# Linformer attention and an MLP mixer: next batch's front half in pieces between channel-mixing blocks, crossbar transposes, TensorE tiles

## The chip, the cores and the metric

One NeuronCore of one Trainium2 chip. The metric is device time in microseconds (us) of one execution, median over runs. PE is TensorE, ACT is ScalarE, DVE is VectorE, POOL is GpSimd, SP is SyncE. "SPq" in a profile line is SP's instruction queue. Matmul results go to tiles in PSUM; the ACT or DVE instruction that reads such a tile out is called its eviction. A crossbar transpose is `dma_start_transpose`, a DMA that transposes on its way.

## The reference, cut to what matters

Eight batches, S = 1024 tokens, 8 heads of 64, model width 512. Inputs are float32; the kernels work in bf16.

```
k_proj = E @ k ; v_proj = F @ v                  # per head, 1024 tokens -> 64 rows
x      = softmax(q @ k_proj.T / 8) @ v_proj      # heads side by side: 1024 x 512
h      = relu(x.T @ w_tok1) @ w_tok2             # token mixing: 1024 -> 256 -> 1024
u      = x + h.T
out    = u + relu(u @ w_ch1) @ w_ch2             # channel mixing: 512 -> 1536 -> 512
```

I call attention and token mixing the front half of a batch, channel mixing the back half.

## The kernel before

The front half of batch b+1 is written in front of the mixing of batch b. PSUM is one pool of eight banks.

```
psA = tile_pool(name="psA", bufs=8, space=PSUM)

def attention(b):
    ... loads of k, v, q, one DMA per head, POOL queue, float32 -> bf16 ...
    for hp in range(HP):                                 # q: copy, 64 TensorE transposes a batch ...
        nc.any.tensor_copy(out=q2_sb[:, hp], in_=q_sb[...])
    ...     nc.tensor.transpose(qt_ps[...], q2_sb[:, hp, si, :, :]..., ident)
    ...     nc.vector.tensor_copy(out=qT_sb[...], in_=qt_ps)
    for si in range(NSI):                                # v projection, 64 of 128 columns used
        nc.tensor.matmul(vproj_ps, FT_sb[:, si, :], v_sb[:, :, si, :], ...)
    for si in range(NSI):                                # then k projection
        nc.tensor.matmul(kproj_ps, ET_sb[:, si, :], k_sb[:, :, si, :], ...)
    for sj in range(2):
        for hp in range(HP):                             # scores: two 64x64 tiles at once, exp on ACT
            ...
        for hp in range(HP):                             # outputs and, in separate matmuls, denominators
            nc.tensor.matmul(dn_ps[...], lhs, bd_ones, ...)
            nc.tensor.matmul(ou_ps[:, ss, :], lhs, vbd_sb[:, hp, :], ...)
            ... reciprocal, multiply -> x_sb ...

def mixer(b, x_sb):
    ... token mixing: 16 + 16 matmuls of 512 columns; u_sb = u_ps + x_sb on DVE ...
    ... u: 32 TensorE transposes, evicted to uT_sb by DVE ...
    ... channel mixing: 96 matmuls -> gT_ps, relu; 96 matmuls -> g2_ps; add u, store ...

xs[0] = attention(0)
... weight loads, POOL queue ...
for b in range(B):
    if b + 1 < B:
        xs[b + 1] = attention(b + 1)
    mixer(b, xs[b])
```

The softmax here doesn't subtract the row's maximum and nothing guards it: scores larger than these inputs give would overflow.

## Time and profile before

571.1 us (median of 3 runs, 571.06 to 571.5).

The page of the kernel before: busy time of PE with its share and instruction count; then PE's busy share and the granted PE clock, in tenths, over 40 equal slices of 14.3 us.

```profile
PE 509.8 (89%) x3120; PEld 259.4 (45%) x3120; DVE 210.4 (37%) x524; ACT 175.9 (31%) x288; POOL 110.9 (19%) x212
...
PE   1540889999999999998999999999999999999997
...
PEclk9975889999999999999999999999999999999999
```

PE is the bound after the first six slices. In the first four it is mostly idle, and in slices three to six the granted clock is lowered (0.5 to 0.8).

The chain of waits of the kernel before, in order of time (start us, length us, what):

```profile
65.69 4.79 DMA q_sb<-in_q_dram
70.57 1.05 ACT q_sb L99
74.44 4.15 PE h_ps L198 x16
...
85.20 20.96 PE gT_ps L233 x96
106.16 20.73 PE g_ps L242 x96
126.92 0.69 DVE o_sb L247
...
149.83 20.96 PE gT_ps L233 x96
```

Channel mixing of batch 0 starts at 85.2 us, because PE meets the attention of batch 1 first and waits there for its q. From then on a batch takes 149.83 - 85.20 = 64.6 us, of which 41.7 are the two channel-mixing loops.

Stretches of the kernel before: the start, then one batch. Columns: stretch, its length, busy time and count for PE, PEld, DVE, ACT, POOL, then PE clock, DMA share (packet times of queues that overlap add up, so it can exceed 1), GB/s.

```profile
0.00:85.20 85.20, 40.72 (x345) 26.02 (x346) 33.85 (x107) 19.00 (x27) 56.91 (x110) 0.82 1.16 193
85.20:149.80 64.60, 62.69 (x390) 31.71 (x388) 25.76 (x64) 21.89 (x36) 15.28 (x29) 1.00 0.48 93
```

In one batch PE is busy 62.7 of 64.6 us. A faster batch therefore needs less PE work, not only better overlap.

### The profile page before, as it was taken

Reading aid. Unit: us, or ns where it says so; the run is one execution under the profiler, and the core shown is the slowest. Engines: PE = TensorE matmul, PEld = TensorE weight load, DVE = VectorE, ACT = ScalarE, POOL = GpSimd, SP = SyncE. Lnnn points to the kernel's source line nnn. Section 1 sums busy time; section 2 is a strip of 40 time slices with the busy share of each in tenths; the row PEclk is TensorE's granted clock in tenths of the full one; section 3 lists DMA queues with packets and bytes.
Section 4 is the critical chain, followed back from the end, with each engine's and each line's share of the span. In section 5 each row is a group of like instructions: output and inputs, shape, how many; then the busy total and the mean of one; then the engine's idle time right before and its main releaser. Section 6 shows DMA issues by size and latency. Waiting matters only on the chain.

```text
span 570.8 us, 7698 instructions
## 1 busy us (share of the span) xinstructions
PE 509.8 (89%) x3120; PEld 259.4 (45%) x3120; DVE 210.4 (37%) x524; ACT 175.9 (31%) x288; POOL 110.9 (19%) x212
## 2 busy tenths in 40 slices
PE   1540889999999999998999999999999999999997
PEld 0330454454544454445544454445544454445443
DVE  1440571137502572028602563027601563025012
ACT  0221336305260235304260235404261034500720
POOL 8608871006200360006200260000000000000000
PEclk9975889999999999999999999999999999999999
DMA  9999992129502390028601391020001200020012
GB/s 135 208 208 202 201 201 44 38 92 151 91 0 79 102 186 4 27 103 134 109 1 73 94 185 19 20 102 28 1 1 69 80 2 0 18 94 38 1 55 92
DMA packets 39555, 46.90 MB, mean 82 GB/s; under 512 B 4192, under 2 KB 30304, under 8 KB 39520
## 3 DMA queue, kind: packets, MB, share of 16 engines
q0 software_dynamic: 30304, 29.63, 32.4%
q1 hardware_dynamic: 9216, 16.78, 7.5%
q8 instruction: 24, 0.39, 0.3%
q14 instruction: 11, 0.09, 0.1%
HBM read 59.24 MB, written 16.78 MB: 133 GB/s over the span
## 4 chain that ended last, share of the span: by engine, by line
PE 71%; DVE 14%; DMA 6%; POOL 5%; issue 2%; ACT 1%; DVEq 0%; ACTq 0%; POOLq 0%
PE gT_ps L233 29%; PE g_ps L242 29%; DVE u_sb L213 6%; PE h_ps L198 5%; DMA wc_sb<-in_moe_w_ch_dram 4%; DVE qT_sb L114 2%; PE ou_ps L178 2%; PE ut_ps L219 2%; POOL v_sb L90 2%; POOL q_sb L94 2%; PE u_ps L209 2%; POOL k_sb L89 1%; DVE x_sb L183 1%; PE dn_ps L175 1%; DVE vbd_sb L128 1%
## 5 line engine op out<-in xcount | busy, mean ns | idle before, releaser
L233 PE MATMUL gT_ps<-uT_sb,wc_sb 128*128 128x512 bf16 x768 | 169.0, 379 | 0.0
L242 PE MATMUL g_ps<-wc_sb,gT_sb 128*128 128x512 bf16 x768 | 167.1, 379 | 0.0
L238 ACT ACTIVATE gT_sb<-gT_ps 128x512 bf16<-128x512 f32 x184 | 109.0, 597 | 111.6 <-PE gT_ps L233 110.5
L247 DVE TENSOR_TENSOR o_sb<-g_ps,u_sb 128x512 f32<-128x512 f32 x64 | 44.3, 692 | 267.7 <-PE g_ps L242 267.7
L242 PEld LDWEIGHTS <-gT_sb 128*128 128x128 bf16 x768 | 75.1, 98 | 90.7
L233 PEld LDWEIGHTS <-wc_sb 128*128 128x128 bf16 x768 | 74.8, 98 | 90.7 <-issue 3.8
L90 POOL DMA_DIRECT2D v_sb<-in_v_dram x64 | 34.7, 545 | 203.2 <-PE vproj_ps L120 188.5
L99 ACT COPY q_sb<-q_sb 128x1024 bf16<-128x1024 bf16 x23 | 23.1, 1044 | 133.8 <-PE qt_ps L109 109.8
L166 ACT ACTIVATE attnT_sb<-sco_ps 128x512 bf16<-128x512 f32 x64 | 33.0, 602 | 61.2 <-PE sco_ps L161 61.2
L109 PE MATMUL qt_ps<-ident,q_sb 128*128 128x128 bf16 x256 | 19.5, 242 | 34.4 <-ACT q_sb L99 34.4
L213 DVE TENSOR_TENSOR u_sb<-u_ps,x_sb 128x512 bf16<-128x512 f32 x64 | 39.0, 683 | 21.2 <-PE u_ps L209 21.2
L183 DVE TENSOR_TENSOR x_sb<-ou_ps,rdn 128x512 bf16<-128x512 f32 x64 | 41.7, 681 | 1.7
L89 POOL DMA_DIRECT2D k_sb<-in_k_dram x64 | 34.6, 554 | 14.9 <-DMA wc_sb<-in_moe_w_ch_dram 6.8
L94 POOL DMA_DIRECT2D q_sb<-in_q_dram x64 | 34.0, 534 | 10.1 <-issue 5.3
L109 PEld LDWEIGHTS <-q_sb 128*128 128x128 bf16 x256 | 17.6, 109 | 37.1 <-ACT q_sb L99 35.5
L114 DVE COPY qT_sb<-qt_ps 128x512 bf16<-128x512 bf16 x64 | 23.0, 417 | 19.2 <-PE qt_ps L109 19.1
L175 PE MATMUL dn_ps<-bd_ones,attnT_sb 128*128 128x2 bf16 x256 | 27.4, 171 | 2.8 <-ACT attnT_sb L166 1.5
L178 PE MATMUL ou_ps<-vbd_sb,attnT_sb 128*128 128x128 bf16 x256 | 29.8, 221 | 0.0
L198 PE MATMUL h_ps<-x_sb,wt_sb 128*128 128x512 bf16 x128 | 29.7, 386 | 0.0
L209 PE MATMUL u_ps<-hT_sb,wt_sb 128*128 128x512 bf16 x128 | 28.9, 379 | 0.0
L175 PEld LDWEIGHTS <-attnT_sb 128*128 128x128 bf16 x256 | 20.0, 96 | 16.2 <-ACT attnT_sb L166 10.8
L219 PE MATMUL ut_ps<-ident,u_sb 128*128 128x128 bf16 x256 | 21.5, 221 | 5.1 <-DVE u_sb L213 4.6
(46 smaller groups left out, 260.0 us busy)
## 6 DMA issues: line engine op xcount, KB each, us to landing
out_dram<-o_sb SPq DMA_DIRECT2D x64, 256.0 KB, 2.0
k_sb<-in_k_dram POOLq DMA_DIRECT2D x64, 128.0 KB, 4.9
v_sb<-in_v_dram POOLq DMA_DIRECT2D x64, 128.0 KB, 4.9
q_sb<-in_q_dram POOLq DMA_DIRECT2D x64, 128.0 KB, 4.9
wc_sb<-in_moe_w_ch_dram POOLq DMA_DIRECT2D x2, 1536.0 KB, 18.8
wt_sb<-in_moe_w_tok_dram POOLq DMA_DIRECT2D x2, 512.0 KB, 7.4
E_sb<-in_E_dram POOLq DMA_DIRECT2D x1, 128.0 KB, 3.1
F_sb<-in_F_dram POOLq DMA_DIRECT2D x1, 128.0 KB, 3.4
```

What stands on the lines that cost most here:

```text
L90: nc.gpsimd.dma_start(out=v_sb[:, h, :, :], in_=v[b, h].rearrange(rr, p=P))
L94: nc.gpsimd.dma_start(out=q_sb[:, h, :, :], in_=q[b, h].rearrange("(p si) d -> p si d", p=P))
L175: nc.tensor.matmul(dn_ps[:, 2 * ss : 2 * ss + 2], lhs, bd_ones, start=True, stop=True)
L178: nc.tensor.matmul(ou_ps[:, ss, :], lhs, vbd_sb[:, hp, :], start=True, stop=True)
L183: nc.vector.tensor_tensor(out=x_sb[:, sj * 4 : sj * 4 + 4, h0 * D : (h0 + 2) * D] .rearrange("p s (j d) -> p s j d", j=2), in0=ou_ps.rearr ...
L198: nc.tensor.matmul(h_ps, wt1_sb[:, sc, tc_i * P : (tc_i + 1) * P], x_sb[:, sc, :], start=(sc == 0), stop=(sc == SC - 1),)
L209: nc.tensor.matmul(u_ps, wt2_sb[:, tc_i, sc::NSI], hT_sb[:, tc_i, :], start=(tc_i == 0), stop=(tc_i == TC - 1),)
L213: nc.vector.tensor_add(out=u_sb[:, sc, :], in0=u_ps, in1=x_sb[:, sc, :])
L233: nc.tensor.matmul(gT_ps, wc1_sb[:, dc, cc * P : (cc + 1) * P], uT_sb[:, dc, s_lo : s_lo + S2], start=(dc == 0), stop=(dc == DMC - 1),)
L238: nc.any.tensor_relu(out=gT_sb[:, cc, s_lo : s_lo + S2], in_=gT_ps)
L242: nc.tensor.matmul(g2_ps, gT_sb[:, cc, sc * P : (sc + 1) * P], wc2_sb[:, cc, :], start=(cc == 0), stop=(cc == CC - 1),)
L247: nc.vector.tensor_add(out=o_sb, in0=g2_ps, in1=u_sb[:, sc, :])
```

## The change

Intent: cut the front half into 24 small units and issue one after every one or two blocks of four channel-mixing matmuls, so that their evictions hide; move the transposes of q and u from PE to the DMA crossbar; put the k and v projections in two column tiles that run at once and the scores in four 64x64 tiles; get the denominators from a column of ones in the output matmul. PSUM is split: three buffers for channel mixing (`psC`), two double ones for scores and outputs (`psA`), one for everything else (`psS`).

```diff
-    psA = tile_pool(name="psA", bufs=8, space=PSUM)
+    psC = tile_pool(name="psC", bufs=3, space=PSUM)
+    psA = tile_pool(name="psA", bufs=2, space=PSUM)     # two banks each
+    psS = tile_pool(name="psS", bufs=1, space=PSUM)
...
+    loaded = {0: load(0, 4)}          # k, v, q; POOL queue
+    ... weight loads ...
+    loaded[1] = load(1, 2)
...
-    nc.tensor.transpose(qt_ps[...], q2_sb[...], ident); nc.vector.tensor_copy(...)
+    def front_units(b):
+        for h in range(0, H, H // 2):                   # two transposes of 128x2048, on SP
+            nc.sync.dma_start_transpose(out=qT[:, h : h + H // 2]..., in_=q_sb[:, h : h + H // 2]...)
...
+        def kv_proj():
+            kv_ps = psS.tile([P, H, D], F32, tag="s", name="kv_ps")
+            for si in range(NSI):
+                nc.tensor.matmul(kv_ps[0:KP], ET_sb[:, si, :], k_sb[:, :, si, :], ...)
+                nc.tensor.matmul(kv_ps[KP : 2 * KP], FT_sb[:, si, :], v_sb[:, :, si, :], ...)
+        ... k_transpose, scores(hp), attend(h), token1(t) ...
+        def token2(si):
+            u_ps = psS.tile([P, DM], F32, tag="s", name="u_ps")
+            ... two matmuls, u_sb = u_ps + x_sb ...
+            if si % NJ == NJ - 1:                       # after the 4th and the 8th: on SP too
+                nc.sync.dma_start_transpose(out=uT[i]..., in_=u_sb[:, i * NJ : (i + 1) * NJ]...)
...
+    for unit in front_units(0):
+        unit()
     for b in range(B):
-        if b + 1 < B:
-            xs[b + 1] = attention(b + 1)
-        mixer(b, xs[b])
+        if b + 2 < B:
+            loaded[b + 2] = load(b + 2, 2)
+        units = front_units(b + 1) if b + 1 < B else []
+        blocks = back_blocks(b)                         # 48 blocks of 4 matmuls
+        first = 12 if b == 0 else 2
+        ... after each block, the units that are due ...
```

## The prediction

> **What bounds the kernel now.** TensorE. The page's first part has PE busy 509.8 us (89%) of 570.8, and the chain of waits is 71% PE, 14% DVE. In order of time the chain repeats every 64.6 us (from 126.9 to 191.5): the two channel-mixing loops 20.96 + 20.73 us (matmuls 216 ns apart); attention of the next batch 12.9; token mixing with the transposes of u 10.0. In the channel-mixing stretch PE is 100% busy, in the attention stretch 11.6 of 12.9 us, in token mixing 9.4 of 10. So little is idle: the gain must come from PE work removed, and from short bubbles. The first channel-mixing matmul starts only at 85.2 us, because PE meets attention(1) before mixing(0) in its order and waits there for q of batch 1 (the copy of it starts at 70.6); the clock is 0.67 to 0.71 there.
>
> **Costs, per batch, from the trace.**
> Removed: transposes of q 1.9 us and of u 2.2 us with their DVE bubbles (now DMA transposes); half of the k and v projections (they run one after the other, 3.6 us; in two column tiles 1.8); the denominator matmuls (a pair of denominator and output takes about 80 ns, a 130-column one alone about 60); waits for evictions in attention, about 1.3 us, and 0.6 in token mixing. The scores already run two 64x64 tiles at once (both start at 133.71); four quadrants halve 1.75 us to 0.9.
> Kept: 41.7 channel, 6.9 token mixing (32 x 216 ns).
> Estimate of the new batch: 41.7 + 6.9 + 1.8 (projections) + 0.6 (k transposed) + 0.9 to 1.7 (scores) + 2.4 (output) + about 1.2 for some ten changes of tile shape (0.1 us each, as between the last output matmul and the next score at 136.6) = 55.5 to 56.3 us instead of 64.6.
>
> **Will the transposes hide?** Each moves 128x2048 bf16, 512 KB. The Trainium skill ("DMA: Bandwidth & Descriptors", Latency and other measured facts) gives 261 GB/s for such a transpose, so about 2 us plus as much fixed; I estimate 4 to 8 us beside the loads; nothing in this trace shows it. In the instruction order the transposes of q stand nearly a batch ahead of their scores, and after the fourth token-mixing block some 11 us of matmuls come before the first that needs u transposed. So they should hide, except at the start.
>
> **Start.** Loads of k, v, q end near 20 us (weights follow until 43). Then q transposes, scores, eight output steps of about 1 us each (two buffers), token mixing with one buffer (8 x 1.4 us), and a transpose of u: channel mixing(0) should start near 53 us (48 to 60) instead of 85, since attention(1) now comes inside it.
>
> **Sum.** 53 + 7 x 56 + 42.5 (last batch has nothing between) + 3 = 490.5 us. Range 474 to 513. Faster by over 2%: 0.95; same 0.03; slower 0.02.
>
> **What would show it.** Period 55 to 57 us between the same blocks of successive batches; PE busy near 95% from 60 us on; channel matmuls still 216 ns apart; k and v projection pairs starting together; four scores starting together; PE's waits for transposed q only in the first batch, for transposed u under 1 us per batch; ACT near 45% with all the relus, not limiting.
>
> **What would make it wrong.** Transposes at 12 us or more each (four per batch), so that the first channel matmul waits each batch: up to 60 us per batch, 520 in all. The Trainium skill ("TensorEngine Tiling (Array Packing)", Key Properties) says that changing the tiling mode drains TensorE; if it costs 0.3 us rather than 0.1, 15 us more. One buffer for projections and token mixing stalling PE in order. A start held to 65 us or more by transposes queued behind the weight loads.

## The result, and the profile after

The changed kernel takes 520.0 us (median of 4 runs, 518.87 to 520.71) against 571.1 us for the kernel before (median of 4, the three runs above among them). The ratio is 0.910, 95% interval 0.909 to 0.911. Ratios here and below are the mean time of one kernel's runs over the mean of the other's runs of the same rounds, so not quite the ratio of the medians. Executions over 1.5% slower than the fastest of the same kernel are left out of the means. The change is clearly faster, but the time lies outside the predicted range of 474 to 513 us.

The page after, same lines as before (slices of 12.9 us):

```profile
PE 449.0 (87%) x2384; PEld 209.1 (40%) x2384; DVE 163.0 (31%) x300; ACT 163.2 (32%) x265; POOL 49.0 (9%) x72
...
PE   1300751999999999999999999999999999999997
...
PEclk9999975999999999999999999999999999999999
```

From slice eight on PE has no visible gap. The start has not become shorter, and it is emptier: PE is busy 24.4 us of its 88.1, against 40.7 of 85.2 before (the stretches below).

The chain of waits after:

```profile
12.05 9.96 DMA q_sb<-in_q_dram
...
22.29 19.96 DMA wc_sb<-in_moe_w_ch_dram
...
42.54 20.19 DMA q_sb<-in_q_dram
...
62.75 7.01 SPq L133
...
69.81 11.81 SPq L133
...
81.66 6.39 DMA uT_172<-u_sb
...
88.09 1.01 PE g_ps L254 x2
...
145.35 3.45 PE g_ps L254 x16
...
199.93 3.45 PE g_ps L254 x16
```

Read from the top: the loads of batch 0, then the weights, then q of batch 1 (landed at 62.7), then two instructions of line 133 on SP (the transposes of q), and only then the transpose of u that the first channel-mixing matmul needs. That matmul starts at 88.1 us, later than the 85.2 before. The steady state is as good as hoped: 199.93 - 145.35 = 54.6 us a batch.

Stretches after: start, batch 0, one steady batch, the last batch (same columns).

```profile
0.00:88.10 88.10, 24.40 (x119) 11.02 (x120) 16.76 (x39) 7.79 (x10) 27.98 (x44) 0.90 1.18 190
88.10:145.35 57.25, 56.92 (x299) 26.37 (x299) 20.04 (x36) 20.51 (x33) 6.14 (x9) 0.97 0.99 183
145.35:199.93 54.58, 54.37 (x298) 25.52 (x296) 19.99 (x36) 20.20 (x33) 4.45 (x6) 1.00 0.66 135
472.80:517.90 45.10, 41.41 (x192) 18.58 (x190) 6.22 (x9) 14.33 (x24) 0.00 (x0) 1.00 0.14 55
```

So the span is 88.1 + 57.25 + 6 x 54.57 + 45.1 = 517.9 us. The prediction had 53 + 7 x 56 + 45.5. Steady batches are 1.4 us shorter than predicted, the start is 35 us longer.

SP's queue in the changed kernel, in order of time:

```profile
20.77 60.85 SPq L133 DMA_TRANSPOSE qT<-q_sb  x4
81.66 4.21 SPq L229 DMA_TRANSPOSE uT_172<-u_sb  x1
```

Four transposes of q stand in front of the first transpose of u: two of batch 0 and two of batch 1. The source has it the other way round: `front_units(0)` runs to its end, with both transposes of u, before `front_units(1)` issues the first transpose of q of batch 1. The order on a queue is the build's, so it has to be read from the trace. PE's scores of batch 0, with the idle time in front of them and what ended it:

```profile
37.96 1.07 PE L183 MATMUL s_ps<-qT,kT 64*64 64x512 bf16 x8 [12.41 <-DMA qT<-q_sb]
...
50.69 0.64 PE L183 MATMUL s_ps<-qT,kT 64*64 64x512 bf16 x4 [11.66 <-DMA qT<-q_sb]
```

The loads of q of batch 0 were in by 22 us, but its first half was transposed only at 38 and its second at 50.7. I had put 4 to 8 us on one such transpose.

### The profile page after: what moved, and what is told of

It is laid out like the page before. It is cut to its first block, busy times and chain, and to the rows that moved or that the text cites. A ratio compares the mean times of both kernels' runs of the same rounds, so it can differ in the third digit from the quotient of the medians.

```text
span 517.9 us, 5765 instructions
## 1 busy us (share of the span) xinstructions
PE 449.0 (87%) x2384; PEld 209.1 (40%) x2384; DVE 163.0 (31%) x300; ACT 163.2 (32%) x265; POOL 49.0 (9%) x72
## 4 chain that ended last, share of the span: by engine, by line
PE 78%; DMA 12%; SPq 4%; ACT 3%; DVE 1%; POOL 1%; issue 1%; POOLq 0%; ACTq 0%
PE o_ps L265 32%; PE g_ps L254 29%; DMA q_sb<-in_q_dram 6%; PE u_ps L222 5%; PE h_ps L213 5%; DMA wc_sb<-in_moe_w_ch_dram 4%; SPq L133 4%; PE kv_ps L151 2%; PE o_ps L195 2%; PE s_ps L183 2%; DMA k_sb<-in_k_dram 1%; ACT gT L258 1%; DMA uT_172<-u_sb 1%; DVE kp_sb L156 1%; ACT kp_sb L157 1%; PE kt_ps L168 1%
## 5 line engine op out<-in xcount | busy, mean ns | idle before, releaser
L258 ACT ACTIVATE gT<-g_ps 128x512 bf16<-128x512 f32 x192 | 113.1, 600 | 224.8 <-PE g_ps L254 224.5
L265 PE MATMUL o_ps<-wc_sb,gT 128*128 128x512 bf16 x768 | 182.3, 379 | 0.0
L265 PEld LDWEIGHTS <-gT 128*128 128x128 bf16 x768 | 72.6, 98 | 80.1 <-issue 2.6
L272 DVE TENSOR_TENSOR o_sb<-o_ps,u_sb 128x512 f32<-128x512 f32 x64 | 44.2, 691 | 78.1 <-PE o_ps L265 78.1
L188 ACT ACTIVATE a_sb<-s_ps 128x1024 bf16<-128x1024 f32 x32 | 32.0, 1031 | 50.8 <-PE s_ps L183 50.6
L203 DVE TENSOR_TENSOR x_sb<-o_ps,rdn 128x512 bf16<-128x512 f32 x64 | 44.2, 691 | 2.2
L183 PE MATMUL s_ps<-qT,kT 64*64 64x512 bf16 x128 | 12.5, 423 | 24.3 <-DMA qT<-q_sb 24.1
L75 POOL DMA_DIRECT2D k_sb<-in_k_dram x18 | 13.5, 750 | 150.4 <-PE kv_ps L152 137.9
L195 PEld LDWEIGHTS <-a_sb 128*128 128x128 bf16 x256 | 20.2, 102 | 17.7 <-DVE x_sb L203 3.1
L222 PEld LDWEIGHTS <-wt_sb 128*128 128x128 bf16 x128 | 18.5, 145 | 21.2 <-issue 11.1
L151 PE MATMUL kv_ps<-k_sb,ET_sb 128*64 128x512 bf16 x64 | 17.2, 413 | 9.8 <-DMA k_sb<-in_k_dram 9.8
L80 POOL DMA_DIRECT2D q_sb<-in_q_dram x18 | 13.2, 739 | 101.7 <-DMA qT<-q_sb 91.9
L213 PEld LDWEIGHTS <-wt_sb 128*128 128x128 bf16 x128 | 13.0, 101 | 18.4 <-issue 4.6
## 6 DMA issues: line engine op xcount, KB each, us to landing
k_sb<-in_k_dram POOLq DMA_DIRECT2D x14, 512.0 KB, 9.7
v_sb<-in_v_dram POOLq DMA_DIRECT2D x14, 512.0 KB, 11.5
q_sb<-in_q_dram POOLq DMA_DIRECT2D x14, 512.0 KB, 8.7
```

What stands on the lines that cost most here:

```text
L151: nc.tensor.matmul(kv_ps[0:KP], ET_sb[:, si, :], k_sb[:, :, si, :], start=a, stop=z)
L183: nc.tensor.matmul(s_ps[dst * KP : (dst + 1) * KP, h % 2, :], kT[rows, h, :], qT[rows, h].rearrange("p j s -> p (j s)"), start=True, stop= ...
L188: nc.scalar.activation(out=a_sb, in_=s_ps, func=ACT.Exp, scale=scale)
L195: nc.tensor.matmul(o_ps[:, j // 2, (j % 2) * 2 * D1 : (j % 2 + 1) * 2 * D1], a_sb[:, h % 2, j * P : (j + 1) * P], vb[:, h // 2, h % 2].rea ...
L203: nc.vector.tensor_tensor(out=x_sb[:, :, h * D : (h + 1) * D].rearrange("p (n c) d -> p n c d", n=2), in0=o4[:, :, :, 0:D], in1=rdn[:, :, ...
L213: nc.tensor.matmul(h_ps, wt1_sb[:, si, t * P : (t + 1) * P], x_sb[:, si, :], start=(si == 0), stop=(si == NSI - 1),)
```

## The experiments

**Two causes for the start, and the rivals.** Theory A has two parts. One is order: the first transpose of u (its four blocks of u are ready at 72.5 us, the end of DVE's fourth addition, shown below) waits in SP's in-order queue behind transposes of batch 1, whose q lands at 62.7. The other is contention: a crossbar transpose is slow while the POOL-queue loads run. The rivals: the volume of the loads sets the start whatever the order (B), or these transposes are slow by themselves (D). The fourth addition in the changed kernel:

```profile
71.79 0.69 DVE L226 TENSOR_TENSOR u_sb<-u_ps,x_sb 128x512 bf16<-128x512 f32 x1 [0.85 <-PE u_ps L222]
```

### e1_ut_first: u before q of batch 1

```diff
-        for h in range(0, H, H // 2):
-            nc.sync.dma_start_transpose(...)            # q
+        behind = tc.issue_after(last_uT[0].ins) if b == 1 else nullcontext()
+        with behind:                                    # issue order only, no wait
+            for h in range(0, H, H // 2):
+                nc.sync.dma_start_transpose(...)
```

> The two transposes of q of batch 1 are queued on SP behind both transposes of u of batch 0; nothing else changes. Theory A (the start is late because the first u transpose stands in SP's in-order queue behind transposes that wait for the load of q of batch 1, and because transposes are slow beside the loads): the first u transpose issues near 73 us (the fourth block of u is ready at 74 in the changed kernel) instead of 81.7, the first channel matmul starts at 80 to 86 us instead of 88.1, and the total is 512 to 518 instead of 520, since q of batch 1 then lands later. Rival B (the start is bound by the volume of the loads, whatever the order): first channel matmul stays at 88, total 520.

Measured: 515.1 us, ratio to the kernel before 0.901 (0.8995 to 0.9025). PE's first channel-mixing matmul:

```profile
82.52 1.01 PE L257 MATMUL g_ps<-uT,wc_sb 128*128 128x512 bf16 x2 [6.49 <-DMA uT<-u_sb]
```

It starts 5.6 us earlier and the kernel is 5 us faster, in the range of A; B is refuted as the whole cause. But the transpose of u, issued at 71.4 us, took 11.1 us to land, against 6.4 in the changed kernel: over 9 us less waiting in the queue won only 5.6. Order alone is the smaller part.

### e2_hold: no loads beside the transposes of q of batch 0

```diff
+    gate = nc.gpsimd.tensor_copy(out=wt1_sb[:, 0, 0:2], in_=qT0[...])   # weight load must wait for it
+    with tc.issue_after(gate.ins):                                      # and all later loads with it
         ... weight loads, loaded[1] = load(1, 2) ...
```

> All loads behind q of batch 0 wait until q of batch 0 is transposed (a two-element copy that the first weight load must overwrite). Theory A: without loads beside them the two transposes of q land about 3.7 us after issue, both by 31 us, instead of 38.0 and 50.7; attention of batch 0 starts near 30 us; but the first u transpose still stands behind one that waits for q of batch 1, which now lands some 9 us later (near 72), so the first channel matmul is at 85 to 97 us and the total 517 to 529: little or no gain. Rival B: 9 us lost on the loads and nothing won, start at 97, total 529. Rival D (these transposes are slow by themselves, or slow while the start is cold): they still land 13 us apart.

Measured: 520.6 us, ratio 0.911 (0.910 to 0.912): no gain, as A said. SP's queue and PE's scores of batch 0:

```profile
20.38 5.54 SPq L92 DMA_TRANSPOSE qT<-q_sb  x2
65.00 7.32 SPq L149 DMA_TRANSPOSE qT<-q_sb  x1
72.38 11.37 SPq L245 DMA_TRANSPOSE uT<-u_sb  x1
```

```profile
25.69 1.07 PE L199 MATMUL s_ps<-qT,kT 64*64 64x512 bf16 x8 [0.78 <-DVE kT L190]
27.70 0.64 PE L199 MATMUL s_ps<-qT,kT 64*64 64x512 bf16 x4 [0.94 <-DMA qT<-q_sb]
```

Without loads beside it the second half of q is there at 27.7 us instead of 50.7, so these transposes are not slow by themselves: D is refuted. The 23 us won are then lost again, in the queue and beside the held-back loads: u of batch 0 is ready at 49.5 us, waits until 72.4 behind a transpose of batch 1 (whose q landed at 65.0), and its own transpose then takes 16.1 us, landing at 88.5.

### e3_both: both edits

> Both edits together. Theory A: q transposed by 31 us, u of batch 0 ready near 52, first channel matmul at 55 to 66 us; then the scores of batch 1 wait up to 10 us for q of batch 1; total 495 to 508. Rival B: total 525 or more.

Measured: 516.0 us (four runs from 511.5 to 518.3; the profiled one is the slowest), ratio 0.902 (0.897 to 0.907). A's range was missed. The first channel-mixing matmul started at 69.2 us instead of 55 to 66, since now the transpose of u, issued at 50.6, ran beside the held-back loads and took 18.5 us:

```profile
69.18 1.01 PE L273 MATMUL g_ps<-uT,wc_sb 128*128 128x512 bf16 x2 [13.91 <-DMA uT<-u_sb]
```

The second transpose of u and then q of batch 1 came late in the same way. Batch 0 then lasted 72.3 us (141.51 - 69.18) instead of 57.25, and at its end PE waited 8.1 us for u of batch 1, whose transpose took 15.0 us to land. So 19 us won at the start became 4 us of the total. My expectation had counted the contention for q and forgotten it for u. Holding loads back only moves the contention.

### e4_pe_b0: batch 0 transposed on PE

```diff
+        def q_transpose(h):
+            t_ps = psS.tile([P, NJ, P], BF16, tag="s", name="t_ps")
+            for j in range(NJ):
+                nc.tensor.transpose(t_ps[:, j], q_sb[:, h, 2 * j : 2 * j + 2, :]..., ident)
+            nc.vector.tensor_copy(out=qT[:, h], in_=t_ps)
+        ... u_transpose(si) likewise; both as further units, for b == 0 only ...
```

> q and u of batch 0 alone are transposed on TensorE as in the kernel before; all other batches keep the DMA transposes; loads as in the changed kernel. Theory A: q transposed by 28 us, first channel matmul at 50 to 57 us, scores of batch 1 wait 5 to 15 us for their transposed q, which lands at 70 to 82 beside the loads; total 490 to 503. Rival B: start stays above 80, total above 515.

Measured: 494.6 us, ratio 0.866 (0.864 to 0.868). The first channel-mixing matmul starts at 61.8 us (I expected 50 to 57), and the scores of batch 1 did not wait for q at all (I expected 5 to 15 us):

```profile
61.84 1.91 PE L277 MATMUL g_ps<-uT,wc_sb 128*128 128x512 bf16 x4
```

The same loads run in the same order, so B is refuted a second time. What keeps the start above 57 looks, in PE's timeline, like a chain through the single PSUM buffer, with the granted clock lowered (the page shows 0.5 and 0.6 in slices four and five); the runs from e11 on test the buffer.

### e6_small: smaller load packets beside the same transposes

How do loads slow a transpose? The Trainium skill ("DMA: Bandwidth & Descriptors", Queues, rings and completion order) says that a DMA engine serves its queues in turn, one packet at a time (whether the profile's packets are the page's, no run shows). The queues of the changed kernel from 21 to 38 us (packets, MB, share of the time of 16 engines), while the first transpose of q ran:

```profile
q0 software_dynamic: 2627, 2.73, 95.7%
q1 hardware_dynamic: 2271, 0.57, 27.5%
```

The two queues had nearly as many packets each, but the loads (q0) moved 2.73 MB and the transposes (q1) 0.57 MB, 34 GB/s. That is what taking turns looks like: a 256 B transpose packet waits for a load packet of about 1 KB (2.73 MB / 2627), about 99 ns (95.7% x 16 x 17 us / 2627). A transpose of 128x2048 bf16 has 2048 such packets, 128 an engine, so an estimate from these numbers is 128 x 99 ns x 2627/2271 = 14.7 us. Measured are 17.2 us from issue for the first and 12.7 more for the second. In a quiet stretch, 243 to 248 us, a transpose of u of the same size lands after 3.7 us:

```profile
q1 hardware_dynamic: 2216, 0.77, 60.1%
...
uT_1314<-u_sb SPq DMA_TRANSPOSE x1, 3.7
```

The test is to keep the bytes and shrink the load packets:

```diff
-    for c in range(0, DC, DC // 4): ... wc1_sb[:, :, c : c + DC // 4] ...
+    for c in range(0, DC, P):       ... wc1_sb[:, :, c : c + P] ...
-    for c in range(0, CC, CC // 4): ... wc2_sb[:, c : c + CC // 4] ...
+    for c in range(0, DM, P):       ... wc2_sb[:, :, c : c + P] ...
```

> The two channel-mixing weight matrices are loaded in pieces of 128 columns (runs of 512 B read, 256 B written, instead of 768 B and 1 KB written): same bytes, smaller packets beside the transposes of q of batch 0. Theory A1 (transpose and load packets alternate on each DMA engine, so that each 256 B transpose packet waits for one load packet): the transposes of q land earlier, the first scores start at 30 to 34 us instead of 38.0 and the third pair of heads at 38 to 45 instead of 50.7, though the weights land later. Rival A2 (the engines share bytes, or the fabric is simply full): the transposes land no earlier, 38 and 50 or later.

Measured in one look: the queues of this kernel from 21 to 38 us, then PE's scores.

```profile
q0 software_dynamic: 4517, 2.01, 89.5%
q1 hardware_dynamic: 4156, 1.05, 47.5%
```

```profile
32.56 1.07 PE L183 MATMUL s_ps<-qT,kT 64*64 64x512 bf16 x8 [8.45 <-DMA qT<-q_sb]
38.73 0.64 PE L183 MATMUL s_ps<-qT,kT 64*64 64x512 bf16 x4 [5.09 <-DMA qT<-q_sb]
```

The packet counts are again nearly equal, a load packet (now 445 B on average) takes 54 ns, and the second transpose follows the first after 6.2 us instead of 12.7. Both scores start in the ranges of A1, and A2 (the engines share bytes) falls. The total, 512.0 us, is one run of unknown state, and the build also placed u of batch 0 ahead of q of batch 1 on SP in this kernel, so I draw nothing from the total.

### e11_psC0, e12_psC0_q1, e13_kv1_late, e15_kv1_late_q1dma: towards a better start

All four start from e4 and give the small units of batch 0 the three channel-mixing PSUM buffers, idle then. The e12 and e13 kernels also transpose q of batch 1 on PE (`b < 2`); e13 and e15 issue the projections of batch 1 only behind the first twelve channel-mixing blocks of batch 0.

```diff
+    spare = lambda b: psC if b == 0 else psS            # e11, e12, e13, e15
-            kv_ps = psS.tile([P, H, D], F32, tag="s", name="kv_ps")    # and kt_ps, h_ps, u_ps, t_ps
+            kv_ps = spare(b).tile([P, H, D], F32, tag=spare_tag(b), name="kv_ps")
...
+                behind = tc.issue_after(last_g[0].ins) if b == 0 and done == 0 else nullcontext()
+                with behind:                            # e13, e15
                     units[done]()
```

> As the run with TensorE transposes for batch 0 alone, and the projections, token mixing and transposes of batch 0 take the three PSUM buffers of channel mixing, which are idle then, instead of the single one. The start is then no longer a one-buffer chain: token mixing of batch 0 takes 7 to 9 us instead of 16 and the first channel matmul starts at 50 to 56 us instead of 61.8; the scores of batch 1 may now wait for their transposed q (0 to 6 us). Total 484 to 491 instead of 494.6. If the start is bound by the loads instead, no change: 494.

> As the run before it, with q of batch 1 transposed on TensorE too, so that nothing of the first two batches waits for a crossbar transpose beside the loads. Adds 32 transposes, about 2 us. If the scores of batch 1 waited for q, 2 to 5 us faster than the run before it (481 to 488); if they did not, about 2 us slower.

Both missed: 499.8 us (ratio 0.875, 0.873 to 0.877) and 499.4 us (ratio 0.872, 0.867 to 0.877; one of its four runs at 493.9), slower than e4. PE's timeline suggests the reason: with more buffers the build had put the projections of batch 1 in front of channel mixing of batch 0, and PE waited there 5.3 us for k and 1.9 us for v of batch 1 (e11; 3.9 and 1.9 in e12), and did the rest of the projections and all transposes of u first. Channel mixing started at 64.9 and 65.9 us. In e11 the scores of batch 1 also waited 5.3 us for transposed q; in e12 that wait is gone, without gain. First the wait for k in e11, then the start in e12:

```profile
51.11 0.64 PE L169 MATMUL kv_ps<-k_sb,ET_sb 128*64 128x512 bf16 x1 [5.33 <-DMA k_sb<-in_k_dram]
```

```profile
65.87 10.52 PE L279 MATMUL g_ps<-uT,wc_sb 128*128 128x512 bf16 x48
```

> As the run with both q of batches 0 and 1 and u of batch 0 on TensorE and the spare PSUM buffers for batch 0 (499.4 us), but the projections of batch 1 are issued on TensorE only behind the first twelve blocks of channel mixing of batch 0. In that run TensorE met the projections of batch 1 first and waited some 10 us for the load of k of batch 1. If that order is what ate the gain, the first channel matmul starts at 52 to 57 us instead of 65.9 and the total is 484 to 491; if the loads bound the start in another way, it stays at 494 or more.

> As the run before it, but q of batch 1 keeps its crossbar transposes, beside the loads of batches 1 and 2. First channel matmul at 52 to 57 as there; transposed q of batch 1 lands at 70 to 90, so the scores of batch 1 wait 5 to 18 us: total 490 to 504, that is 3 to 15 us slower than the run before it. If transposes beside loads no longer matter by then: the same time.

Measured: 491.2 us for e13 (ratio 0.859, 0.858 to 0.860), 0.2 us above its range, and 493.9 us for e15 (ratio 0.863, 0.862 to 0.865). The "some 10 us" in the expectation was a misreading: the longest wait for k in the list is that of batch 0; the right figure for batch 1 is the 3.9 us above. The order did eat the gain all the same: with that one order changed, e13 starts channel mixing 12 us earlier than e12, at 53.6 us. (That the prediction had 53 is chance: it was made for another kernel.) It is an in-order queue again, this time PE's. How the 12 us divide between waits, lowered clock and work moved behind was not separated.

```profile
53.64 10.52 PE L280 MATMUL g_ps<-uT,wc_sb 128*128 128x512 bf16 x48
...
114.96 5.30 PE L280 MATMUL g_ps<-uT,wc_sb 128*128 128x512 bf16 x16 [4.09 <-DMA uT<-u_sb]
```

The second line shows what is left: batch 0 lasts 61.3 us instead of 57.25, and at its end PE waits 4.1 us for the transposed u of batch 1. In e15 the scores of batch 1 waited 6.4 us for transposed q, and it is 2.7 us slower than e13. That is just under the 3 us expected. e15 also bears on what held e4: in both traces the projections of batch 1 come behind the first channel-mixing blocks, so what differs up to there is the PSUM buffers (and the order the build made with them), and channel mixing starts at 53.2 us instead of 61.8. The total is hardly better than that of e4 (493.9 against 494.6), since PE then waits for q, and 2.5 us for u, of batch 1. e13 gives correct results and beats both kernels; it is the version I would keep.

### e5_pe_all: no crossbar transposes

The edit of e4, for all batches.

> q and u of all batches transposed on TensorE, in pieces between the channel-mixing blocks, through the one-buffer PSUM pool; no crossbar transposes at all. Where the steady gain comes from: 64 transposes of 128 columns per batch cost about 56 to 60 ns each, 3.6 to 3.9 us a batch, so if the interleaving hides the evictions the period goes from 54.6 to 58 to 60 us. Theory A (start): first channel matmul near 62 us as in the run with TensorE transposes for batch 0 alone, so total 62 + 7 x 59 + 45 = about 520 (508 to 528): start and steady state cancel. If the DMA transposes carry the steady gain in other ways (evictions stall TensorE), the period is over 61 and the total over 535.

Measured: 527.0 us, ratio 0.921 (0.919 to 0.923). The first channel-mixing matmul is at 61.4 us and a steady batch lasts 302.4 - 242.9 = 59.5 us (first channel-mixing matmul to first); total, start and batch are as expected. So the crossbar transposes are worth 4.9 us in each steady batch, and cost some 27 us at the start.

### e7_kv_serial: the pairing of the projections

```diff
             for si in range(NSI):
                 nc.tensor.matmul(kv_ps[0:KP], ET_sb[:, si, :], k_sb[:, :, si, :], ...)
+            for si in range(NSI):
                 nc.tensor.matmul(kv_ps[KP : 2 * KP], FT_sb[:, si, :], v_sb[:, :, si, :], ...)
```

> The eight matmuls of the k projection are issued before the eight of the v projection, so that the two column tiles no longer alternate and cannot overlap. If the pairs run at once (as both starts of 203.31 and 203.32 us say), each batch pays 8 x 216 ns = 1.7 us more: period 56.3 us, total 530 to 535. If the pairing gained nothing: period 54.6, total 520.

Measured: 525.3 us, ratio 0.918 (0.916 to 0.920), between the two expectations. The timeline of PE shows why:

```profile
204.66 1.27 PE L151 MATMUL kv_ps<-k_sb,ET_sb 128*64 128x512 bf16 x5
205.55 0.40 PE L154 MATMUL kv_ps<-v_sb,FT_sb 128*64 128x512 bf16 x1
205.76 0.38 PE L151 MATMUL kv_ps<-k_sb,ET_sb 128*64 128x512 bf16 x1
...
206.22 1.24 PE L154 MATMUL kv_ps<-v_sb,FT_sb 128*64 128x512 bf16 x5
207.40 3.63 PE L256 MATMUL g_ps<-uT,wc_sb 128*128 128x512 bf16 x16
```

Issued as eight k and then eight v matmuls (the built program has them in this order on PE), the first v matmul is recorded before the last three k matmuls, in the other column tile, and three pairs still overlap. The stretch takes 2.74 us; 16 matmuls one after the other would take 3.46, the paired version takes 1.85 (203.31 to 205.16 in the changed kernel). A batch lasts 55.4 us instead of 54.6. So the pairing is real, and this edit did not undo it fully: the gain of 1.7 us a batch is supported by the two ends (3.6 us in the kernel before, 1.85 after); this run alone shows 0.9 of it.

### e8_apart: no interleaving

```diff
+        with tc.issue_after(last_mm[0].ins):            # PE's last matmul of the batch before
+            for unit in units:                          # the whole front half of batch b+1
+                unit()
+        ... then all blocks of batch b, issued behind the last unit ...
```

> No interleaving: the attention and token-mixing units of the next batch are issued on TensorE in one stretch ahead of the channel mixing of this batch (issue order only; pools, transposes and tiles as in the changed kernel). Theory: with one buffer for projections and token mixing and two for scores and outputs, the units alone are a latency chain: about 8 x 1.35 us for the second token matmul, 8 x 0.84 for the attention outputs, 5 for the first token matmul, 8 for projections and scores, some 31 us instead of 13 us of matmuls; period about 72 us, total 600 to 650, slower than the kernel before (64.6 us a batch). Rival (the gain is the removed TensorE work, interleaving hides only the 2 us of bubbles seen before): period 57 to 60, total 535 to 560.

Measured: 685.8 us, ratio 1.196 (1.190 to 1.202), beyond the expected 600 to 650. One batch:

```profile
240.70:320.00 79.30, 64.16 (x296) 28.41 (x298) 20.04 (x36) 20.72 (x33) 4.46 (x6) 0.83 0.46 93
```

The same 296 matmuls now take 79.3 us. The latency chain through one or two PSUM buffers was foreseen (about 72 us a batch); what I left out is the clock that the gaps bring down, here to a mean of 0.83. The Trainium skill ("TensorE: Matmul & The Clock Gate", Part 1) says that the array falls back to half rate after an idle window of about 3.4 us. Here shorter gaps were enough: from 265 to 270 us the granted clock was 0.95, from 270 to 275 it was 0.50, and no gap between matmuls in these 10 us was longer than 0.8 us. How much of the 7 us beyond 72 is the clock was not separated. So these small PSUM pools depend on the interleaving; whether larger pools would do without it was not tested.

## Why the prediction was right or wrong

- **Bound now: right.** PE bound the kernel before, and a batch got shorter by the PE work removed: PE's busy time in a batch went from 62.7 to 54.4 us.
- **Costs per batch: right, a little high.** 55.5 to 56.3 us predicted, 54.6 measured. An output step of four 130-column matmuls takes 0.22 us (from 214.78 to 215.00 in PE's timeline), so eight take 1.8 us against my 2.4, and a change of tile shape costs about 0.1 us, as estimated: the last projection pair starts at 204.85, the next matmul at 205.16, 0.31 us against 0.216.
- **Transposes hide in steady state: right.** They land after 3.7 us (u) in quiet stretches, and in the changed kernel PE waited for transposed q twice in all (24.1 us), both in batch 0, and for transposed u once (11.0 us), also of batch 0.
- **"Start": this step failed.** Channel mixing was put at 53 us (48 to 60); it came at 88.1. Two things in it were wrong. The first is a cost, "4 to 8 us beside the loads": the estimate took 261 GB/s from the Trainium skill and let the loads at most double the time. Beside loads the transposes moved 34 GB/s, one landed after 17.2 us, and q was complete at 50.7 us instead of about 28 (20 plus at most 8), some 23 us late. e2 shows that the loads cause it, the packet counts and e6 show how.
- **The second is a path, the queue.** "In the instruction order the transposes of q stand nearly a batch ahead of their scores" was read as an advantage. On an in-order queue it is also a delay for everything behind: u of batch 0 was ready at 72.5 and issued at 81.7 us. It stood there because the build had put q of batch 1 in front of it, against the order of the source. e1 shows it by moving it, and e2 more starkly (ready at 49.5, issued at 72.4). The list of what would make it wrong named a start held by transposes "queued behind the weight loads", but with too little weight (its range ended at 513) and not quite this way: the transposes of q ran beside the loads, turn by turn, and u stood behind other transposes. That its "520 in all", for slow transposes in every batch, is also what was measured is chance: steady batches took 54.6 us.
- The two make up about 23 + 9 of the 35 us. The other 3 were not separated; the first eight token-mixing matmuls, 3.57 us against 2.01 for the next eight, are in them. The two do not act apart: taking away one of them won 5.6 us (e1) or nothing (e2), both 19 us (e3), and taking the transposes of batch 0 off the DMA queues 26 us of the start (e4).

## What to carry to other kernels

A crossbar transpose was cheap when the DMA queues were quiet (3.7 us) and several times slower beside bulk loads with larger packets (17.2 us), in step with the packets of both queues; where the start is full of loads, as here, try the transposes on PE. An early place in an in-order queue is only good for the instruction that has it: before moving waits to a queue, list from the built kernel's trace what stands behind them and when each is ready. Units with one PSUM buffer needed other matmuls between them, to hide evictions and to keep the clock up (54.6 us a batch with them, 79.3 at a clock of 0.83 without).

## What the Trainium skill lacked or had wrong

- "DMA: Bandwidth & Descriptors" gives 261 GB/s for a crossbar transpose with a non-contiguous middle dimension, more for a contiguous one, and in another table, on correctness, asks nothing of a transpose next to ordinary DMAs. For speed, here it was 3.7 us from issue to landing for 512 KB in a quiet stretch, and 17.2 us beside POOL-queue loads (34 GB/s from 21 to 38 us). The page's account of packets served in turn fits it; the page does not draw the consequence.
- The same page does not say that other DMAs lengthen the time for which issuing a transpose holds SP's queue: 1.3 us for u in quiet stretches, up to 17.0 us for q beside loads in the changed kernel.
- "TensorE: Matmul & The Clock Gate", Part 3, says that matmuls start and end in strict order. In e7 a matmul of the free column tile is recorded as starting at 205.55 us, ahead of three issued before it for the busy tile (205.76 the first of them), and the stretch is shorter (2.74 us) than if the starts had kept the order of issue: then only the last k and the first v could pair, 15 steps of 0.216 us, 3.24.
- "TensorEngine Tiling (Array Packing)", Key Properties, says that a change of tiling mode drains TensorE but not what that costs; here it was about 0.1 us.
